# Linear attention with a gated FFN on one core: later loads held behind the first tile, eps on POOL, the last sum in two halves, and another search for the order

## The chip, the cores and the metric

The kernel runs on one core of one Trainium2 chip. The metric is the device time of an execution in microseconds, here the median of several runs. The engines are TensorE (PE, with its weight loads shown apart as PEld), VectorE (DVE), ScalarE (ACT), GpSimd (POOL) and SyncE (SP), which issues all DMAs.

## The reference

```python
xn = layernorm(A_x)                              # 2048 x 512, eps 1e-5
q, k, v = split(xn @ A_wqkv)                     # 32 heads of 16
pq, pk = phi(q), phi(k)                          # where(t > 0, t + 1, exp(t)) + 1e-6
kv = sum_s pk^T v ; z = sum_s pk                 # per head
o = (pq @ kv) / (pq . z + 1e-6)
s = o @ A_wo
g = silu((gelu(xn @ w_gate) * (xn @ w_up)) @ w_down)   # 512 -> 1792 -> 512
y = A_x + s * g
```

All is float32. (The FFN's input is the normalised x as well.)

## The kernel before

**Tiles.** The 2048 rows are 16 tiles of 128 tokens (`x`, normalised `xn`, transposed on PE into the bank `pt`). Each number is split into a high part that PE takes in its fast float format (a cast on ACT: `Xh`, `kq`, `xnh`, `hh`, `dwh`) and a low rest (a subtraction on DVE: `Xl`, `kq`, `xnl`, `hl`, `dwl`); a product is then three matmuls, `mm3`, lines 364 to 366. The larger products run by a scheme with seven block products instead of eight (`prod`, `fprod`), whose sums of blocks (`T`, `tmp`) are made on POOL.

**Stages.** (1) Normalise, transpose, products for k and q, `phi` of both; q is written to `q_d`, and `gacc` gathers pk and xn into the four banks `gps`. The first four tiles use plain products (`plain`), later ones the scheme. (2) From about 118 us the FFN of the second half of the tokens (`quad`, banks `FX`, `FY`, `FZ`), whose down products go to the banks `d` and are added to `acc` in groups of units (`down`). (3) From about 330 us the attention part: `kv`, `pm`, and for each of 16 tiles a transpose `ptq`, a cast `pqTh` and the product `sps`. (4) From about 410 us the FFN of the first half, and at the end `finish0`: silu of `acc`, times `s` (tile `fs`, loaded from `s_d`), plus x (tile `fx`), and the store.

**What sets the order.** Nothing is issued while the code runs: `do` records each operation with its engine, an estimated duration and what it must wait for. `Plan.order` then puts them in sequence. PE's order is written by hand as a list of keys (`pe_keys`), from which the planner may run ahead by 6 us (`AHEAD`). From PE's turn each operation gets a latest time `late`; `forward` goes through the program and takes on each engine the ready operation with the smallest `late`. Then 400 rounds (`ROUNDS`) shift `late` at random around one of PE's planned waits and keep what doesn't end later. The result is one fixed order for each engine, so a waiting instruction holds up everything behind it on its engine; SP's DMAs stand in one queue too.

**The first tile.** `load_next` and `dma` queue x and wqkv by turns: the first x tile, half of `wk1`, the second x tile, and so on, none waiting for anything. `ln` makes the statistics (`st`, `mv`) on DVE, adds eps (`ve`, line 504) on DVE, raises to -0.5 on POOL (`rstd`, line 506) and normalises on DVE (line 510). PE runs 15 warm-up matmuls on ones, then the transposes.

**The end.** The last tile's sum (`j == 7`) is made by 12 matmuls of 512 columns into one bank; DVE then adds it to `acc` in two halves of 256 columns, and silu, product and addition of x follow by halves. For tiles 0 to 5 the addition of x stands on POOL, for 6 and 7 on DVE.

## Time and profile before

| what | us |
|---|---|
| runs | 632.27, 632.03, 629.70 (median 632.03) |
| the profiled execution | 629.64, its span 627.6 |
| PE busy in the span | 616.1 |
| DVE, ACT, POOL busy | 422.2, 321.2, 247.9 |

A row of the timeline gives the start, the duration, the engine, the line and the operation, and in brackets how long the engine had been idle and what ended that. The ends of matmuls are modelled: in an unbroken row one starts every 0.227 us though each is shown with 0.39. Busy time of PE therefore tells little; the idle time and the steps between starts tell where it waited. A table by stretches gives for each window its length and the busy time of PE, PEld, DVE, ACT and POOL.

### The profile page before, as it was taken

To read this page: it belongs to the slowest core of one execution; us is meant where nothing else is said; L and a number is where in the kernel's file an instruction comes from. 1 tells how busy PE (TensorE), PEld (TensorE's weight loads), DVE (VectorE), ACT (ScalarE), POOL (GpSimd) and SP (SyncE) were. 2 spreads that over 40 slices of the span, in tenths; PEclk is the share of its full clock that TensorE was granted. 3 is DMA by queue.
4 is the path that set the end of the run, shared out by engine and by line. 5 is a ranking of instruction groups with operands and counts; after the bars stand their busy time and mean duration, and the time that the engine had idled before them with its cause. 6 is when DMAs were issued, how large, how long until landed. Compare 5 with 4: busy or idle time off the path is not lost.

```text
span 627.6 us, 7822 instructions
## 1 busy us (share of the span) xinstructions
PE 616.1 (98%) x2780; PEld 506.0 (81%) x2780; DVE 422.2 (67%) x644; ACT 321.2 (51%) x571; POOL 247.9 (40%) x243
## 2 busy tenths in 40 slices
PE   7999999999999999999999999999999999999995
PEld 6878788888888888888888787888888888888884
DVE  6999998688746743762459689967566527723554
ACT  6677777797565622650345322266656316612431
POOL 2465554456644530360035433135534404300142
PEclk9999999999999999999999999999999999999999
DMA  6239921136121210220069544872221202000173
GB/s 239 80 124 299 298 68 38 65 102 201 44 72 54 56 46 34 67 68 0 34 201 359 199 131 148 289 251 67 68 65 36 68 34 68 0 1 34 34 206 130
DMA packets 52439, 68.67 MB, mean 109 GB/s; under 512 B 2864, under 2 KB 31792, under 8 KB 52400
## 3 DMA queue, kind: packets, MB, share of 16 engines
q1 hardware_dynamic: 52400, 68.17, 33.9%
q8 instruction: 22, 0.36, 0.2%
q14 instruction: 17, 0.14, 0.1%
HBM read 49.28 MB, written 18.87 MB: 109 GB/s over the span
## 4 chain that ended last, share of the span: by engine, by line
PE 94%; DVE 3%; ACT 1%; issue 0%; POOL 0%; DVEq 0%; ACTq 0%; POOLq 0%
PE FX L364 8%; PE FX L365 8%; PE FX L366 8%; PE d L365 8%; PE d L366 8%; PE d L364 8%; PE FZ L365 4%; PE FZ L366 4%; PE FZ L364 4%; PE sps L366 2%; PE sps L364 2%; PE sps L365 2%; PE gps L366 2%; PE gps L364 2%; PE gps L365 2%; PE FY L365 2%
## 5 line engine op out<-in xcount | busy, mean ns | idle before, releaser
L847 POOL TENSOR_TENSOR h<-h,g 128x512 f32<-128x512 f32 x42 | 62.1, 1477 | 173.3 <-DVE h L356 173.3
L364 PE MATMUL d<-dwh,hh 128*128 128x512 f32 x224 | 87.8, 392 | 0.0
L364 PE MATMUL FX<-Xh,w 128*128 128x512 f32 x224 | 87.5, 391 | 0.1
L366 PE MATMUL FX<-Xh,w 128*128 128x512 f32 x224 | 87.2, 389 | 0.0
L366 PE MATMUL d<-dwh,hl 128*128 128x512 f32 x224 | 87.2, 389 | 0.0
L365 PE MATMUL d<-dwl,hh 128*128 128x512 f32 x224 | 87.2, 389 | 0.0
L365 PE MATMUL FX<-Xl,w 128*128 128x512 f32 x224 | 87.2, 389 | 0.0
L356 POOL TENSOR_TENSOR tmp<-raw 128x256 f32<-128x256 f32 x56 | 49.1, 890 | 85.1 <-DVE w L356 70.3
L885 DVE TENSOR_TENSOR acc<-acc,d 128x512 f32<-128x512 f32 (+1 forms) x49 | 32.8, 674 | 52.5 <-PE d L366 52.1
L350 ACT COPY fu<-FX 128x512 f32<-128x512 f32 x56 | 32.9, 587 | 54.3 <-PE FX L366 53.7
L350 ACT CAST hh<-h 128x512 fp32r<-128x512 f32 x56 | 34.5, 620 | 46.4 <-PE d L365 27.0
L364 PEld LDWEIGHTS FX<-Xh,w 128*128 128x128 f32 x224 | 42.0, 188 | 10.0 <-ACT fu L350 1.4
L364 PEld LDWEIGHTS d<-dwh,hh 128*128 128x128 f32 x224 | 42.1, 188 | 8.9 <-issue 0.2
L365 PEld LDWEIGHTS d<-dwl,hh 128*128 128x128 f32 x224 | 42.1, 188 | 8.8 <-issue 0.2
L366 PEld LDWEIGHTS d<-dwh,hl 128*128 128x128 f32 x224 | 42.0, 188 | 8.7
L366 PEld LDWEIGHTS FX<-Xh,w 128*128 128x128 f32 x224 | 42.0, 188 | 8.7
L365 PEld LDWEIGHTS FX<-Xl,w 128*128 128x128 f32 x224 | 42.0, 188 | 8.7
L356 DVE TENSOR_TENSOR w<-tmp,w 128x512 fp32r<-128x512 f32 x56 | 42.0, 772 | 9.8 <-ACT w L350 9.8
L356 DVE TENSOR_TENSOR w<-raw,w 128x512 fp32r<-128x512 f32 (+1 forms) x56 | 45.7, 825 | 3.2 <-ACT w L350 3.2
L356 DVE TENSOR_TENSOR hl<-h,hh 128x512 fp32r<-128x512 f32 x56 | 41.2, 735 | 5.6 <-ACT hh L350 5.6
L364 PE MATMUL FZ<-Xh,w 128*128 128x512 f32 x112 | 43.6, 389 | 0.0
L365 PE MATMUL FZ<-Xl,w 128*128 128x512 f32 x112 | 43.6, 389 | 0.0
(186 smaller groups left out, 1396.8 us busy)
## 6 DMA issues: line engine op xcount, KB each, us to landing
raw<-in_B_w_gate SPq DMA_DIRECT2D x14, 512.0 KB, 3.8
raw<-in_B_w_up SPq DMA_DIRECT2D x14, 512.0 KB, 3.8
draw<-in_B_w_down SPq DMA_DIRECT2D x14, 512.0 KB, 3.3
x<-in_A_x SPq DMA_DIRECT2D x16, 256.0 KB, 3.3
q_d<-qp SPq DMA_DIRECT2D x16, 256.0 KB, 2.2
q<-q_d SPq DMA_DIRECT2D x16, 256.0 KB, 3.0
xh_d<-Xh SPq DMA_DIRECT2D x4, 896.0 KB, 5.9
xl_d<-Xl SPq DMA_DIRECT2D x4, 896.0 KB, 6.4
```

The costliest lines, as they stand in the source:

```text
L350: do("ACT", act(n), lambda o, i: nc.scalar.copy(o, i), dst, src, name=name)
L356: do(eng, c, lambda o, p, q: getattr(e, f"tensor_{op}")(o, p, q), dst, a, b, name=name)
L364: nc.tensor.matmul(ps, wh, mh, start=start, stop=False, skip_group_check=on)
L365: nc.tensor.matmul(ps, wh, ml, start=False, stop=False, skip_group_check=on)
L366: nc.tensor.matmul(ps, wl, mh, start=False, stop=stop, skip_group_check=on)
L847: do("POOL", pool(NC), lambda o, i: nc.gpsimd.tensor_mul(o, o, i), h, g, name="h")
L885: do("DVE", dve(D // n), lambda o, i: nc.vector.tensor_add(o, o, i), acc[p, j][cl], ps[cl], name="acc")
```

## The change

Four edits go together.

1. **Loads.** Only the first x tile, the first half of the k weights (`wk1`) and the second x tile are issued at once. Every later load of the start first has one column of its target overwritten by a copy on POOL (`hold`) from the first tile's statistics, so that the load must wait for these.
2. **eps.** The addition of eps (`ve`) moves from DVE to POOL, for all tiles.
3. **The last sum.** In the last group of the FFN of the first half the tile `j == 7` is made in two halves of 256 columns, each in a bank of its own, with 24 matmuls of 256 columns; the views of `acc` and `fs` have two parts, so that each half is waited for by itself. The addition of x is on DVE for all tiles.
4. **The search.** Instead of 400 rounds, a table (`KEPT`) lists stretches of PE's turn and the seeds that are applied there; a round shifts `late` either along the chain that held up one wait (`chain`) or around it.

```diff
-ROUNDS = 400
+KEPT = [
+    (-1, 12, [300008, 300085, 300320, 300352]),
+    (12, 25, [300005]),
...
+    (605, 9999, [300017, 300018, 300031]),
+]
...
+        for lo, hi, draws in KEPT:
+            for n in draws:
+                best = self.altered(n, lo, hi, pe, *best)
+        return [o for _, o in best[1]]
+
+    def altered(self, n, lo, hi, pe, _, done, late):
+        draw = random.Random(n)
+        for o in self.ops:
+            o.late = late[o]
+        waits = [w for w in self.waits(done) if lo <= w[0] < hi]
+        if not waits:
+            return _, done, late
+        w = draw.choices(waits, [w[1] for w in waits])[0]
+        if draw.random() < 0.5:
+            for o in self.chain(done, w[2]):
+                if draw.random() < 0.7:
+                    o.late -= draw.uniform(0.0, 4.0)
...
+        new = self.forward(pe)
+        return max(t for t, _ in new), new, {o: o.late for o in self.ops}
...
-        do("DVE", 0.1, lambda o, i: nc.vector.tensor_scalar_add(o, i, EPS_LN), ve, mv[:, :, 1])
+        do("POOL", 0.1, lambda o, i: nc.gpsimd.tensor_scalar_add(o, i, EPS_LN), ve, mv[:, :, 1])
...
+    load_next()
+    for k in range(2):
+        dma(half(wk1, k), ext(wqkv_k[:, k, D:2 * D]), 256)
+    load_next()
+
+    t0 = tokens[0][0]
+    mv0 = ln_stats(t0)
+
+    def hold(v):
+        do("POOL", 0.1, lambda o, i: nc.gpsimd.tensor_copy(o, i), v, mv0[:, 0, 0:1], name="hold")
+
+    for k in range(2):
+        hold(half(wk2, k)[:, 0:1])
+        dma(half(wk2, k), ext(wqkv_k[:, 2 + k, D:2 * D]), 256)
+    for _ in range(2):
+        t = xq.pop(0)
+        xs[t] = U("x", range(0, 4), f"x{t}")
+        hold(xs[t][:, 0:1])
+        dma(xs[t], ext(x[t * P:(t + 1) * P, :]), 256)
...
+    ln(t0, mv=mv0)
...
+    def halves(p, units_, j):
+
+        return 2 if p == 0 and units_ == groups[-1] and j == 7 else 1
...
+            for c in range(m):
+                ps = bank(ring("down", [5, 6, 7]), f"d{p}_{units_[0]}_{j}{c}", (P, D // m))
+                cs = slice(c * D // m, (c + 1) * D // m)
...
-            tt("POOL" if j < 6 else "DVE", "add", sr[cl], sr[cl], xr[cl], w)
+            tt("DVE", "add", so, so, xr[:, i * w:(i + 1) * w], w)
```

What this does to the order is seen in the built programs, at three places.

**The start, POOL.** Before, from the last of the set-up to the third power (`mask` belongs to the attention, `rstd` is the root of the variance):

```order
L382 MEMSET zacc 128x512
L955 MEMSET mask_114 128x128
L956 AFFINE_SELECT mask_114<-mask_114 128x128
L506 TENSOR_TENSOR rstd_145<-ve_142,neg_half 128x1
L506 TENSOR_TENSOR rstd_172<-ve_167,neg_half 128x1
L506 TENSOR_TENSOR rstd_231<-ve_226,neg_half 128x2
```

And now, behind the same set-up:

```order
L539 COPY wk_133<-mv_126 128x1
L521 TENSOR_SCALAR ve_135<-mv_126 128x1
L539 COPY wk_133<-mv_126 128x1
L523 TENSOR_TENSOR rstd_139<-ve_135,neg_half 128x1
L539 COPY x_142<-mv_126 128x1
L539 COPY x_149<-mv_126 128x1
L539 COPY wq_152<-mv_126 128x1 x2
L539 COPY wq_168<-mv_126 128x1 x2
L521 TENSOR_SCALAR ve_180<-mv_176 128x1
L523 TENSOR_TENSOR rstd_185<-ve_180,neg_half 128x1
```

Two copies and the addition stand between the first statistics and the first root, and six copies between the first and the second root.

**The start, DVE.** Before, from the first statistics:

```order
L501 BN_STATS st_134<-x_95 128x6
L502 BN_AGGR mv_140<-st_134 128x2
L504 TENSOR_SCALAR ve_142<-mv_140 128x1
L510 TENSOR_SCALAR xn_149<-x_95,mv_140,rstd_145 128x512
L501 BN_STATS st_152<-x_110 128x6
L502 BN_AGGR mv_163<-st_152 128x2
L504 TENSOR_SCALAR ve_167<-mv_163 128x1
L356 TENSOR_TENSOR Xl_170<-pt_154,Xh_165 128x2x128 x2
L510 TENSOR_SCALAR xn_177<-x_110,mv_163,rstd_172 128x512
L356 TENSOR_TENSOR kq_175<-wk_106,kq_175 128x512 x2
```

And now:

```order
L513 BN_STATS st_124<-x_95 128x6
L514 BN_AGGR mv_126<-st_124 128x2
L527 TENSOR_SCALAR xn_144<-x_95,mv_126,rstd_139 128x512
L403 TENSOR_TENSOR kq_146<-wk_113,kq_146 128x512
L513 BN_STATS st_165<-x_118 128x6
L514 BN_AGGR mv_176<-st_165 128x2
L403 TENSOR_TENSOR Xl_178<-pt_154,Xh_163 128x2x128 x2
L403 TENSOR_TENSOR kq_146<-wk_113,kq_146 128x512
L403 TENSOR_TENSOR kq_146<-wk_133,kq_146 128x512
L513 BN_STATS st_200<-x_142 128x6
L527 TENSOR_SCALAR xn_205<-x_118,mv_176,rstd_185 128x512
```

The first low half of the weights (`kq`) now stands ahead of the second tile's statistics, and the second tile's `xn` behind two more of them and the third tile's statistics. PE's second transpose, which needs that `xn`, stood ahead of all products and now stands behind nine matmuls of the first tile.

**At 44 us, DVE.** Before, around the last `phi` of q (`qp`), whose bank PE's product `Y` takes next:

```order
L356 TENSOR_TENSOR kq_204<-wk_106,kq_204 128x1024
L356 TENSOR_TENSOR kq_259<-s_1_420,kq_204 128x512
L356 TENSOR_TENSOR kq_259<-s_0_430,kq_204 128x512
L356 TENSOR_TENSOR kq_259<-wq_138,kq_259 128x1024
L591 SCALAR_TENSOR_TENSOR qp_557<-q_520,qr_547 128x512
L356 TENSOR_TENSOR Xl_170<-pt_512,Xh_165 128x2x128
```

And now:

```order
L403 TENSOR_TENSOR kq_207<-wk_113,kq_207 128x1024
L657 SCALAR_TENSOR_TENSOR qp_566<-q_524,qr_556 128x512
L403 TENSOR_TENSOR Xl_178<-T_550,Xh_163 128x4x128
L403 TENSOR_TENSOR kq_274<-s_0_434,kq_207 128x512
L403 TENSOR_TENSOR kq_274<-s_1_442,kq_207 128x512
L403 TENSOR_TENSOR kq_274<-wq_152,kq_274 128x1024
```

`qp` has moved ahead of three of the low halves of the weights.

**The end, PE and DVE.** PE near 596 us, before, between the third and the last product into the bank `FX`:

```order
L366 MATMUL FX_5300<-Xh_3776,w_5009 128x512
L364 MATMUL d_5_0_5374<-dwh_5_5195,hh_25_5132 128x512
L365 MATMUL d_5_0_5374<-dwl_5_5200,hh_25_5132 128x512
L366 MATMUL d_5_0_5374<-dwh_5_5195,hl_25_5137 128x512
L364 MATMUL FX_5300<-Xh_3776,w_5009 128x512
```

And now:

```order
L413 MATMUL FX_5312<-Xh_3769,w_5019 128x512
L411 MATMUL d_5_00_5382<-dwh_5_5203,hh_25_5140 128x512
L412 MATMUL d_5_00_5382<-dwl_5_5208,hh_25_5140 128x512
L413 MATMUL d_5_00_5382<-dwh_5_5203,hl_25_5145 128x512
L411 MATMUL d_5_00_5382<-dwh_5_5203,hh_25_5280 128x512
L412 MATMUL d_5_00_5382<-dwl_5_5208,hh_25_5280 128x512
L413 MATMUL d_5_00_5382<-dwh_5_5203,hl_25_5290 128x512
L411 MATMUL FX_5312<-Xh_3769,w_5019 128x512
```

Six matmuls of a down product stand there instead of three. DVE at the very end, before:

```order
L885 TENSOR_TENSOR acc_6_4286<-acc_6_4286,d_5_6_5534 128x512
L1069 TENSOR_TENSOR fs_5490<-fs_5490,acc_6_4286 128x512
L356 TENSOR_TENSOR fs_5490<-fs_5490,fx_5468 128x512
L885 TENSOR_TENSOR acc_7_4311<-acc_7_4311,d_5_7_5552 128x256 x2
L1069 TENSOR_TENSOR fs_5505<-fs_5505,acc_7_4311 128x256
L356 TENSOR_TENSOR fs_5505<-fs_5505,fx_5487 128x256
```

And now:

```order
L956 TENSOR_TENSOR acc_6_4295<-acc_6_4295,d_5_60_5528 128x512
L403 TENSOR_TENSOR fs_3969<-fs_3969,fx_5425 128x512
L1139 TENSOR_TENSOR fs_5501<-fs_5501,acc_6_4295 128x512
L956 TENSOR_TENSOR acc_7_4308<-acc_7_4308,d_5_70_5559 128x256
L403 TENSOR_TENSOR fs_5501<-fs_5501,fx_5483 128x512
L956 TENSOR_TENSOR acc_7_4308<-acc_7_4308,d_5_71_5575 128x256
L1139 TENSOR_TENSOR fs_5517<-fs_5517,acc_7_4308 128x256
L403 TENSOR_TENSOR fs_5517<-fs_5517,fx_5491 128x256
```

The two halves of the last sum are separate now, with the addition of tile 6 between them, and the addition of tile 5 has come over from POOL.

More of the change, by code (lines that the diff above doesn't have):

```diff
@@ L70 @@
 class Op:
-    __slots__ = ("eng", "cost", "lat", "fn", "pre", "suc", "key", "late", "end", "left", "ready", "name", "turn", "port", "kb", "lat0")
+    __slots__ = ("eng", "cost", "lat", "fn", "pre", "suc", "key", "late", "end", "left", "ready", "name", "turn", "port", "kb", "lat0", "no")
 class Plan:
@@ L928, in ffn @@
         assert len(todo) == 1
-        return keys, lambda j: [("D", p, u, j, i) for u in todo[0] for i in range(2)]
+        return keys, lambda j: [("D", p, u, j, i, c) for c in range(halves(p, todo[0], j)) for u in todo[0] for i in range(2)]
     keys1, last1 = ffn(1, lambda p, j: silu(p, j))
```

138 lines of the change are left out of this document (79 added, 59 removed).

## The prediction

> **What bounds the kernel now.** I read the page's head first, then busy times by stretch, then the timeline of PE and the rows around its gaps.
>
> ```profile
> span 627.6 us, 7822 instructions
> PE 616.1 (98%) x2780; PEld 506.0 (81%) x2780; DVE 422.2 (67%) x644; ACT 321.2 (51%) x571; POOL 247.9 (40%) x243
> ...
> 5.00:20.00 15.00, 12.53 (x66) 9.81 (x66) 13.90 (x30) 12.96 (x27) 4.71 (x5) 1.00 0.60 216
> 20.00:44.00 24.00, 23.61 (x108) 19.18 (x106) 23.29 (x42) 16.93 (x31) 14.20 (x13) 1.00 0.29 92
> 44.00:65.00 21.00, 20.43 (x93) 16.19 (x94) 19.63 (x33) 14.46 (x27) 8.23 (x10) 1.00 0.93 282
> ```
>
> PE is the bound: 11.5 us of the span lie outside its busy time, and only these can be won, since no matmul is taken away. In the three stretches (length, then busy PE, PEld, DVE, ACT, POOL) DVE works 56.8 of 60 us: up to 65 us DVE is as tight as PE, and a wait of PE there is work that DVE did too late.
>
> The gaps of PE inside the program, by timeline (start, duration; the bracket is the idle time and what ended it):
>
> ```profile
> 43.41 0.68 DVE L591 SCALAR_TENSOR_TENSOR qp<-q,qr 128x512 f32<-128x512 f32 x1
> ...
> 44.14 0.50 PE L364 MATMUL Y<-kq,Xh 128*128 128x512 f32 x1 [0.53 <-DVE qp L591]
> ...
> 64.05 0.67 DVE L356 TENSOR_TENSOR Xl<-T,Xh 128x512 fp32r<-128x512 f32 x1
> ...
> 64.78 0.50 PE L366 MATMUL X<-kq,Xl 128*128 128x512 f32 x1 [0.43 <-DVE Xl L356]
> ...
> 326.92 0.39 PE L366 MATMUL d<-dwh,hl 128*128 128x512 f32 x1
> ...
> 327.36 0.50 PE L364 MATMUL FX<-Xh,w 128*128 128x512 f32 x1
> ...
> 388.97 0.50 PE L364 MATMUL sps<-M_hi,pqTh 128*128 128x512 f32 x1 [0.29 <-ACT pqTh L350]
> ...
> 596.33 0.59 ACT L350 COPY fu<-FX 128x512 f32<-128x512 f32 x1 [2.13 <-PE FX L366]
> ...
> 596.53 0.39 PE L366 MATMUL d<-dwh,hl 128*128 128x512 f32 x1
> ...
> 596.97 0.50 PE L364 MATMUL FX<-Xh,w 128*128 128x512 f32 x1
> ```
>
> A matmul starts every 0.227 us in an unbroken row (eleven steps from 618.18 to 620.68, quoted with the tail). So the waits are 0.53, 0.43, 0.21 (327.36 less 326.92 and 0.227), 0.29 and 0.21 us. The rest of the 11.5 us is the start and the tail.
>
> **Part 1, the start.** What stands there now:
>
> ```profile
> 3.41 0.69 DVE L501 BATCH_NORM_STATS2 st<-x 128x6 f32<-128x512 f32 x1 [2.35 <-DMA x<-in_A_x]
> ...
> 4.14 0.18 DVE L502 BATCH_NORM_AGGREGATE mv<-st 128x2 f32<-128x6 f32 x1
> ...
> 4.60 0.56 POOL L506 TENSOR_TENSOR rstd<-ve,neg_half 128x1 f32<-128x1 f32 x1 [1.79 <-DVE ve L504]
> ...
> 5.19 0.55 DVE L510 TENSOR_SCALAR xn<-x,mv,rstd 128x512 f32<-128x512 f32 x1 [0.68 <-POOL rstd L506]
> ...
> 6.06 0.60 PE L522 MATMUL pt<-ident,xn 128*128 128x128 f32 x4
> ...
> 6.23 0.69 DVE L501 BATCH_NORM_STATS2 st<-x 128x6 f32<-128x512 f32 x1 [0.49 <-DMA x<-in_A_x]
> ...
> 6.70 0.65 ACT L350 CAST Xh<-pt 128x256 fp32r<-128x256 f32 x2 [0.31 <-PE pt L522]
> ...
> 8.64 0.66 PE L522 MATMUL pt<-ident,xn 128*128 128x128 f32 x4 [1.98 <-DVE xn L510]
> ...
> 12.76 0.70 POOL L506 TENSOR_TENSOR rstd<-ve,neg_half 128x2 f32<-128x2 f32 x1 [4.78 <-DVE ve L504]
> ...
> 13.00 0.50 PE L366 MATMUL k<-kq,b 128*128 128x512 f32 x1 [0.49 <-DVE b L356]
> ...
> 13.34 0.40 PE L364 MATMUL k<-kq,b 128*128 128x512 f32 x1
> ...
> 14.10 0.66 PE L522 MATMUL pt<-ident,xn 128*128 128x128 f32 x4
> ...
> x<-in_A_x SPq DMA_DIRECT2D x16, 256.0 KB, 3.3
> ```
>
> PE idles 1.98 us for the second transpose, which now stands ahead of every product; in the change nine matmuls of the first tile stand ahead of it. Row 13.34 gives a second price: after a wait the next matmul follows after 0.34 instead of 0.227 us, so each wait costs 0.11 more.
>
> The added work is on POOL. Between the aggregate and the power stand two hold copies and the eps addition, then six more copies. No such operation is in the trace, so I bound it. From below:
>
> ```profile
> 56.56 0.74 POOL L356 TENSOR_TENSOR T<-xt,T 128x256 f32<-128x256 f32 x1
> ...
> 612.44 1.29 POOL L356 TENSOR_TENSOR fs<-fs,fx 128x512 f32<-128x512 f32 x1 [1.49 <-DVE fs L1069]
> ```
>
> 256 columns more cost 0.55 us, so what does not depend on columns is 0.74 - 0.55 = 0.19 us. From above, the only one-column operation with inputs, the power, took 0.56. A copy is nearer to the fixed part: I take 0.19. The aggregate ends at 4.32; with 0.09 us to POOL, three operations of 0.19 and the power of 0.56 the root is ready at 5.54, and xn starts at 5.57 instead of 5.19. That 0.38 us hides behind the warm-up matmuls, which hold the first transpose at 6.06 to 6.2 as before. The held loads (second half of wk, two x tiles, wq) leave later, but wk2 is cast only after 8 us. The third x tile queues behind a load that waits for xn and is issued near 6.6; at 3.3 us to land (the page's median for x) it is there before its statistics at about 11.2.
>
> DVE by steps of 0.60 (512 columns), 0.34 (256) and 0.45 (xn) then has: low half of kq 6.0, statistics of the second tile 6.6 (not waited for: fewer loads fly beside it), Xl 7.4, kq 8.1, kq 8.9 (after ACT's cast), statistics 9.5, second xn 10.1 to 10.64. The transpose goes at 10.7 and the first block of products ends near 11.8; the next has its wait for b until 12.3 instead of 13.0. But the third transpose needs the root of two tiles, now with the addition on POOL: aggregate to 12.3, 0.19 + 0.70, xn 13.35 to 13.9, transpose at 13.95 instead of 14.10. Of the 1.98 us PE gets 0.15 at this point, and about 0.4 two blocks later, because the fourth transpose fits between products. I take **-0.3** (bounds -0.8, with the additions at nothing, to +1.2, with 0.56 each, worked out below).
>
> **Part 2, the order up to 65 us.** At 44 DVE did three low halves of kq ahead of qp, whose bank Y needs; in the change qp stands ahead of them and 44.14 is not waited for. At 64.78 two xn, xnl, c, kp and statistics preceded Xl; one xn of 0.45 is gone from there. Together the two waits are 0.53 + 0.43 + 2 x 0.11 = 1.18 us. DVE's work is the same but for the eps additions, so some of it is late elsewhere: I take **-0.8** (bounds -1.2 and +0.5, another wait like the largest of these).
>
> **Part 3, PE's own order later.** At 596 PE put three matmuls between the last product into FX and the next; they last 0.68 us, while the copy fu needs the bank until 596.92. The change puts six there (1.36 us), which covers it. At 327 another product of six stands between. At 388 two transposes stood back to back with their cast behind them; one now stands thirteen rows earlier. These waits are 0.21 + 0.29 + 0.21 + 3 x 0.11 = 1.04 us; I take **-0.9** (bounds -1.04 and 0).
>
> **Part 4, the tail.**
>
> ```profile
> 618.18 0.39 PE L364 MATMUL d<-dwh,hh 128*128 128x512 f32 x1
> ...
> 618.38 0.69 DVE L885 TENSOR_TENSOR acc<-acc,d 128x512 f32<-128x512 f32 x1 [0.64 <-PE d L366]
> ...
> 619.83 0.69 DVE L1069 TENSOR_TENSOR fs<-fs,acc 128x512 f32<-128x512 f32 x1 [0.76 <-ACT acc L895]
> ...
> 620.55 0.69 DVE L356 TENSOR_TENSOR fs<-fs,fx 128x512 f32<-128x512 f32 x1
> ...
> 620.68 0.39 PE L366 MATMUL d<-dwh,hl 128*128 128x512 f32 x1
> ...
> 621.17 0.74 DVE L885 TENSOR_TENSOR acc<-acc,d 128x256 f32<-128x256 f32 x2
> ...
> 623.37 0.42 DVE L356 TENSOR_TENSOR fs<-fs,fx 128x256 f32<-128x256 f32 x1
> ...
> 13.11 0.19 PEld L364 LDWEIGHTS k<-kq,b 128*128 128x128 f32 x1
> ...
> 349.91 3.59 PE L991 MATMUL pm<-mstuff 128*128 128x512 f32 x8
> ```
>
> Twelve matmuls of 512 columns become 24 of 256, each with its own weight load. Two loads can start 0.11 us apart (one goes with 13.00, the next at 13.11), half a matmul streams 0.11, so I take 0.12 each: the last starts at 618.18 + 23 x 0.12 = 620.94 and is done at 621.22. DVE decides, not PE. It now does the sixth tile's addition too (at 619.00, in a free place), the product at 619.83, first half 620.45, addition 620.82, second half 621.42, then product, addition, product, addition at 621.79, 622.25, 622.60 and 623.05, the last 0.32 us ahead of 623.37: **-0.3**. If the 0.19 us of a load cannot overlap with itself, the second half waits until 622.8 and the end is 1.1 us later than now.
>
> [...] No run here shows half-width products yet.
>
> **The sum.** -0.3 - 0.8 - 0.9 - 0.3 = -2.3 us. An order that was not run before will also make waits, and I allow one short one, +0.3: **-2.0**. The profiled execution took 629.64 (span 627.6 and 2.0 around it), which gives 627.6. The other three took 632.27, 632.03 and 629.7: two levels 2.4 us apart, which the trace doesn't explain. I set the change against the mean of the four, 630.9: **628.9 us**; on the median alone it would be 630.0.
>
> **The rivals.** *The waits only move* (chance 0.28): DVE is 95% busy to 65 us, so parts 1 and 2 give nothing and parts 3 and 4 remain: -0.9 - 0.3 + 0.3 = -0.9, 630.0. For it speaks the busy table, against it the plainly non-urgent statistics and kq that stood ahead of urgent rows.
>
> *Holding the loads doesn't help and delays the first tile* (0.14): it lands by 3.41 either way, since its load is first in the queue. With 0.56 us for each small POOL operation xn starts 3 x 0.37 = 1.1 us later than I have it, the third transpose another 0.37, DVE has no slack to make it good: part 1 is +1.2, part 2 nothing, the sum 1.2 - 0.9 - 0.3 + 0.3 = +0.3, 631.2. It loses from about 0.5 us an operation on.
>
> *Half-width products don't run at half the time* (0.06): the slow side. The fp32 products pm took 3.59 / 8 = 0.45 us for 512 columns in each of two passes, 0.45 for 256 in both. At that pace the last half-width matmul starts at 618.18 + 23 x 0.45 = 628.5; the tail is 7.0 us longer and the sum -2.0 + 0.3 + 7.0 = +5.3, 636.2. It turns the whole change slower from about 0.22 us a matmul on, that is when half a width costs as much as a whole one. Against it: products of this type stream 512 columns in 0.227.
>
> *Everything comes* (0.10): all parts at their good bounds, -0.8 - 1.2 - 1.0 - 0.4 = -3.4, 627.5. The forecast keeps 0.42.
>
> **How the numbers follow.** About 0.5%, 3.2 us, is what a measurement of this kernel can tell. Counted from the median 632.03, faster begins at 628.9: half of the forecast, the good case, and a sixth of the moved waits, together 0.38. Slower is the half-width case and a little of the delayed start, 0.08; the rest is 0.54. The range goes from below the good case with the lower level, 626.8, to the delayed start with the upper, 632.6.
>
> **What would show it.** Right: the second transpose of PE no longer has idle time before the first product, no wait is left at qp, at 327, 388 and 597, and the last half-width matmul starts less than 2.9 us after the first. Wrong: small POOL rows of half a microsecond between aggregate and power; DVE idle for a load near 7 or 11 us; new brackets of over 0.3 us on PE between 20 and 130 us; half-width matmuls 0.19 us or more apart; more than 0.1 us lost between PE's end and the last addition.

## The result, and the profile after

The changed kernel took 632.65 us (median of 22 runs, 631.81 to 633.44), the kernel before 631.92 (22 runs beside them, 629.70 to 633.07): a ratio of 1.0017, 95% interval 1.0009 to 1.0026. It is a little slower, and 3.8 us over the forecast of 628.9; the median lies just above the range. In the figures of this document one run of 691.02 us (three moves) and one of 3571.7 us (the kernel before) are left out, since they stand far from all others of their kernels. The profiled execution took 633.17 us, with this head of its page:

```profile
span 631.4 us, 7862 instructions
...
PE 619.1 (98%) x2792; PEld 507.8 (80%) x2792; DVE 427.3 (68%) x641; ACT 320.3 (51%) x571; POOL 244.4 (39%) x254
```

Twelve more matmuls (halves at the end), eleven more rows on POOL. The span is 3.8 us longer than in the first profile of before, and PE is again the bound. The busy times by stretch (length, PE, PEld, DVE, ACT, POOL):

```profile
5.00:20.00 15.00, 12.55 (x60) 9.19 (x60) 11.12 (x23) 10.06 (x21) 5.25 (x14) 1.00 0.65 216
20.00:44.00 24.00, 24.00 (x111) 19.84 (x111) 22.78 (x42) 18.72 (x34) 16.07 (x17) 1.00 0.30 92
44.00:65.00 21.00, 20.66 (x96) 16.46 (x95) 20.76 (x32) 13.92 (x26) 7.98 (x9) 1.00 0.80 234
```

At the start DVE is no longer tight (11.1 of 15 us, 13.9 before): it now has idle time of its own. PE's timeline has the rest:

```profile
7.36 0.60 PE L588 MATMUL pt<-ident,xn 128*128 128x128 f32 x4
...
10.83 0.50 PE L412 MATMUL k<-kq,Xh 128*128 128x512 f32 x1 [0.94 <-DVE kq L403]
12.49 0.66 PE L588 MATMUL pt<-ident,xn 128*128 128x128 f32 x4 [0.22 <-DVE xn L527]
...
16.34 0.66 PE L588 MATMUL pt<-ident,xn 128*128 128x128 f32 x4 [0.59 <-DVE xn L527]
...
24.12 0.39 PE L411 MATMUL q<-a,Xh 128*128 128x512 f32 x1
...
59.19 0.50 PE L411 MATMUL X<-kq,Xh 128*128 128x512 f32 x1 [0.34 <-DVE qp L657]
...
82.80 0.50 PE L411 MATMUL X<-kq,Xh 128*128 128x512 f32 x1 [0.20 <-ACT u L397]
...
107.76 0.50 PE L411 MATMUL X<-kq,Xh 128*128 128x512 f32 x1 [0.42 <-DVE qp L657]
...
140.04 0.50 PE L411 MATMUL FX<-Xh,w 128*128 128x512 f32 x1 [0.98 <-DVE qp L657]
...
421.04 0.50 PE L411 MATMUL FX<-Xh,w 128*128 128x512 f32 x1 [0.83 <-ACT fu L397]
```

The waits of before at 44, 64, 389 and 597 us are gone. In their place are the five last rows, from 59 us on, at places where the profile of before marks no wait. The first transpose starts at 7.36 us, 6.06 in the first profile of before, although its input is ready by 6.31.

Since two runs differ in where they start, I count PE's idle time from its first transpose on: each matmul's start less the start of the one ahead, less 0.227 us for 512 columns (0.12 for 256, 0.09 for each piece of a transpose), summed by stretch. The stretch 165 to 440 us holds some 3 us in every kernel for steps of other shapes. The second column of numbers is the first transpose's start, the last is what is left of the span, the tail among it (span less all columns ahead, less 609 us of work).

| kernel | span | first transpose | to 24 us | 24-72 | 72-100 | 100-165 | 165-440 | 440-610 | left |
|---|---|---|---|---|---|---|---|---|---|
| before, first profile | 627.6 | 6.06 | 3.68 | 2.64 | 0.46 | 0.49 | 3.91 | 0.32 | 1.0 |
| before, second profile (below) | 630.0 | 7.37 | 4.80 | 2.64 | 0.35 | 0.61 | 3.89 | 0.36 | 1.0 |
| changed | 631.4 | 7.36 | 4.44 | 1.52 | 1.64 | 2.77 | 4.05 | 0.00 | 0.6 |
| three moves | 628.9 | 6.69 | 4.44 | 1.63 | 1.59 | 1.50 | 3.36 | 0.01 | 0.7 |
| middle of before | 628.4 | 6.26 | 4.42 | 2.16 | 0.65 | 0.46 | 4.70 | 0.05 | 0.7 |
| middle, moves, no hold | 625.6 | 6.39 | 3.32 | 2.15 | 0.67 | 0.39 | 3.04 | 0.06 | 0.6 |

So the change wins 1.1 us from 24 to 72 us, 0.3 at the end of the middle part and 0.4 in the tail, and loses 1.2 to 1.3 us from 72 to 100 and 2.2 to 2.3 from 100 to 165 us. Between 165 and 440 us a gain and a loss cancel. The start is 0.4 us better or 2.1 worse, by which profile of before it is held against. Most of the 2.1 is the later first transpose; behind it PE is idle 0.76 us more than in the first profile and 0.36 less than in the second.

### The profile page after: what moved, and what is told of

Its sections match the earlier page's. It is cut to its first block, busy times and chain, and to the rows that moved or that the text cites. A ratio compares the mean times of both kernels' runs of the same rounds, so it can differ in the third digit from the quotient of the medians.

```text
span 631.4 us, 7862 instructions
## 1 busy us (share of the span) xinstructions
PE 619.1 (98%) x2792; PEld 507.8 (80%) x2792; DVE 427.3 (68%) x641; ACT 320.3 (51%) x571; POOL 244.4 (39%) x254
## 4 chain that ended last, share of the span: by engine, by line
PE 73%; DVE 2%; ACT 1%; DMA 1%; issue 1%; POOLq 0%; DVEq 0%
PE FX L411 8%; PE FX L413 8%; PE FX L412 8%; PE d L413 7%; PE d L411 7%; PE d L412 7%; PE FZ L411 4%; PE FZ L413 4%; PE FZ L412 4%; PE sps L413 2%; PE sps L411 2%; PE sps L412 2%; PE FY L413 2%; PE FY L411 2%; PE FY L412 2%; PE ptq L1088 1%
## 5 line engine op out<-in xcount | busy, mean ns | idle before, releaser
L411 PE MATMUL d<-dwh,hh 128*128 128x512 f32 (+1 forms) x228 | 88.4, 388 | 0.0
L413 PE MATMUL d<-dwh,hl 128*128 128x512 f32 (+1 forms) x228 | 87.9, 385 | 0.0
L412 PE MATMUL d<-dwl,hh 128*128 128x512 f32 (+1 forms) x228 | 87.9, 385 | 0.0
L403 POOL TENSOR_TENSOR tmp<-raw 128x256 f32<-128x256 f32 x56 | 44.4, 809 | 78.4 <-DVE w L403 62.8
L403 DVE TENSOR_TENSOR w<-raw,w 128x512 fp32r<-128x512 f32 (+1 forms) x56 | 48.4, 874 | 5.4 <-ACT w L397 5.4
L403 DVE TENSOR_TENSOR hl<-h,hh 128x512 fp32r<-128x512 f32 x56 | 44.4, 793 | 7.2 <-ACT hh L397 7.0
L411 PE MATMUL FZ<-Xh,w 128*128 128x512 f32 x112 | 43.7, 390 | 0.0
L413 PE MATMUL FZ<-Xh,w 128*128 128x512 f32 x112 | 43.6, 389 | 0.0
```

The costliest lines, as they stand in the source:

```text
L403: do(eng, c, lambda o, p, q: getattr(e, f"tensor_{op}")(o, p, q), dst, a, b, name=name)
L411: nc.tensor.matmul(ps, wh, mh, start=start, stop=False, skip_group_check=on)
L412: nc.tensor.matmul(ps, wh, ml, start=False, stop=False, skip_group_check=on)
L413: nc.tensor.matmul(ps, wl, mh, start=False, stop=stop, skip_group_check=on)
```

## The experiments

All medians below may be set against 632.65: the lowest run of the kernel before was between 629.51 and 629.75 us in each of the five sets of runs, so the chips agree within 0.3 us, while its median went from 630.4 to 631.9 with the share of its two levels.

**The kernel before, profiled again.** No edit.

> The kernel before, unchanged, profiled a second time, because its times fall on two levels, about 629.7 and 632.3, and its trace shows only the lower one. Theory one (the levels are two starts: the warm-up matmuls run 0.21 us a record until the pace doubles, at a moment that differs from run to run, and the first transpose waits for them): a run near 632 shows the first transpose 1.3 us or more later than 6.06 and a lower mean clock, and from 20 us on PE keeps this distance to the first trace within 0.3 us; a run near 629.7 shows it at 6.0 to 6.2. Theory two (the levels come from later waits, a load or a bank): the first transpose is at 6.1 in either and PE falls behind at a place after 20 us.

The run took 632.09 us, the upper level. Its PE timeline at the start:

```profile
7.37 0.60 PE L522 MATMUL pt<-ident,xn 128*128 128x128 f32 x4
9.95 0.71 PE L522 MATMUL pt<-ident,xn 128*128 128x128 f32 x4 [1.98 <-DVE xn L510]
10.36 0.73 PE L364 MATMUL k<-kq,Xh 128*128 128x512 f32 x1
10.88 0.63 PE L365 MATMUL k<-kq,Xh 128*128 128x512 f32 x1
11.31 0.63 PE L366 MATMUL k<-kq,Xl 128*128 128x512 f32 x1
```

and the windows of 7 to 12 and 12 to 24 us (the number ahead of the last two is the granted clock), first of this run, then of the first profile:

```profile
7.00:12.00 5.00, 3.02 (x17) 2.54 (x16) 3.32 (x7) 4.00 (x10) 0.56 (x1) 0.84 1.01 365
12.00:24.00 12.00, 11.95 (x51) 9.16 (x51) 10.67 (x22) 9.78 (x20) 3.96 (x3) 0.92 0.18 55
```

```profile
7.00:12.00 5.00, 3.36 (x17) 2.87 (x18) 4.92 (x11) 5.00 (x12) 0.56 (x1) 1.00 1.04 395
12.00:24.00 12.00, 11.51 (x54) 8.83 (x53) 11.65 (x26) 10.42 (x21) 5.29 (x4) 1.00 0.17 58
```

The first transpose is 1.31 us later, and after PE's pause of 1.98 us the products start 0.43 us apart instead of 0.227, at a granted clock of 0.84 and then 0.92. By the first q product PE is 2.44 us behind, and it stays 2.4 to 2.5 behind to the end. The two levels are two starts, as theory one had it; of the 2.44 us, 1.31 are the later first transpose (the warm-ups take 6.41 us; 5.11 in the first profile, where they start 0.213 us apart up to 4.39 us and 0.112 from there on), and the rest goes with the lower clock after the pause, where theory one looked for it in the warm-ups alone. The times on record bear this out: of the 108 runs of before for which they give the granted clock, the 58 with 0.998 or 0.999 over the whole run took 629.51 to 631.31 us, the 50 with 0.995 or 0.996 took 631.61 to 633.10. Against the median of the first group (630.1) the changed kernel is 2.5 us slower, against that of the second (632.5) about as fast. The profile that the prediction was made from was of the better start.

**The old search on the new steps.** The table of draws goes, the 400 rounds of before come back.

```diff
-        for lo, hi, draws in KEPT:
-            for n in draws:
-                best = self.altered(n, lo, hi, pe, *best)
+        draw = random.Random(1)
+        for n in range(ROUNDS):
...
```

> The changed kernel with one part undone: the order comes from the search of before (400 draws over the whole run), and held loads, additions on POOL and the tail in halves stay. Theory one (the new order wins 1.4 us to 70 us and about 1 us at 327 to 600, but loses 3.8 us between 70 and 170 us and 0.85 us at 421, by waits of PE for DVE and ACT that it made itself): this order has the product's low half of wd behind qp and c at 140 us, so that wait of 1.15 us is gone, and the qp of 44 us is ahead as in the change; the time is 629.5 to 631.5, at least 1 us below the changed kernel. Theory two (the loss comes from what all orders share, the held loads, the smaller steps on POOL and the clock): the time is that of the changed kernel, 632.65 within 0.5 us.

633.54 us (632.37 to 635.24, ratio to before 1.003, interval 1.0017 to 1.0044). The wait at 140 us fell to 0.25, but others came (1.58 at 12 us, 0.80 at 61, 0.55 at 102), and the one at 421 stayed. Neither theory: the new search is 0.9 us better than the old one on these steps, so the loss is not that a worse search took the place of a better one.

**No hold.** The eight copies are planned but emit nothing.

```diff
-        do("POOL", 0.1, lambda o, i: nc.gpsimd.tensor_copy(o, i), v, mv0[:, 0, 0:1], name="hold")
+        do("POOL", 0.1, lambda o, i: None, v, mv0[:, 0, 0:1], name="hold")
```

> The changed kernel without the hold copies: the later loads leave at once, while PE, DVE, ACT and the order stay word for word; eight one-column copies are gone from POOL. Theory one (the first tile is first in its queue and lands as soon either way; xn waited 0.35 us longer for two more copies, but the warm-up matmuls hold the first transpose): the first statistics start at 3.4 to 3.7 us as in both kernels, the root is ready 0.2 us (one copy row) or more earlier, the second tile lands later or as soon, and the time is within 0.4 us of the changed kernel. Theory two (the held loads make room): the first statistics start 0.3 us or more later and the time is 0.5 us or more longer. Theory three (the hold is what made the start slower): the first q product is 1 us or more earlier than 24.1, and the time 1 us shorter.

632.71 us (632.12 to 633.96): the same. The first statistics start at 3.46 us instead of 3.70, so holding the later loads does not bring the first tile sooner. Theory one.

**eps on DVE.**

```diff
-        do("POOL", 0.1, lambda o, i: nc.gpsimd.tensor_scalar_add(o, i, EPS_LN), ve, mv[:, :, 1])
+        do("POOL", 0.1, lambda o, i: nc.vector.tensor_scalar_add(o, i, EPS_LN), ve, mv[:, :, 1])
```

> The changed kernel with eps added on DVE again, in the same place of the order: DVE has one small row more for each root, POOL one less; PE, ACT and the loads stay. Theory one (an addition of one or two columns costs either engine about 0.2 us, so DVE has 8 x 0.1 to 0.2 us more in the first 90 us, and the hop between the engines is the same): within 0.5 us of the changed kernel, rather longer, 0 to +0.5 us. Theory two (POOL's step is what delays xn and the third transpose): the root chain from aggregate to xn is 0.2 us shorter or more, and the time 0.3 to 0.8 us shorter.

633.45 us (632.97 to 634.43): 0.8 longer. The start is not where it shows. PE waits for xn at 49 us (0.25) and at 63 us, where the changed kernel has no wait,

```profile
63.03 0.63 PE L588 MATMUL pt<-ident,xn 128*128 128x128 f32 x4 [0.53 <-DVE xn L527]
```

and 0.92 instead of 0.42 at 108; the wait of 0.34 at 59 us is gone. Nine such rows of about 0.15 us stand on DVE, some 1.4 us in all, and a little over half of that reaches the kernel's time; DVE is busy 96% of the time from 44 to 100 us. Taking them off DVE is a real gain of the change in this order, of which the prediction counted nothing.

**Three moves.** Four steps of the planned order are moved by hand (step, ahead of or behind which).

```diff
+MOVES = [(819, False, 629), (888, False, 819), (488, True, 483), (1575, True, 1573)]
...
-    for o in plan.order(pe_keys):
+    turn = plan.order(pe_keys)
+    for n, ahead, m in MOVES:
+        o, to = plan.ops[n], plan.ops[m]
+        turn.remove(o)
+        turn.insert(turn.index(to) + (not ahead), o)
+    for o in turn:
         o.fn()
```

DVE of the changed kernel at 138 us, with the low half of wd (dwl) ahead of the row that PE waits for:

```profile
137.56 0.68 DVE L657 SCALAR_TENSOR_TENSOR qp<-c,qr 128x512 f32<-128x512 f32 x1
138.17 1.21 DVE L403 TENSOR_TENSOR dwl<-draw,dwh 128x1024 fp32r<-128x1024 f32 x1
139.30 0.68 DVE L657 SCALAR_TENSOR_TENSOR qp<-X,qr 128x512 f32<-128x512 f32 x1
```

and ACT at 419 us, with the table load and gelu ahead of the copy that empties bank FX:

```profile
418.59 1.28 ACT L885 ACT_TABLE_LOAD   x1
419.88 0.63 ACT L885 ACTIVATE g<-g 128x512 f32<-128x512 f32 x1
420.42 0.57 ACT L397 COPY fu<-FX 128x512 f32<-128x512 f32 x1
```

dwl is first used at 177 us, gelu's result by POOL several microseconds later; neither had to be there.

> The changed kernel with four rows of its order moved by hand and nothing else: at 140 us the 1.2 us low half of wd on DVE goes behind qp and c (and the load that waits for it behind it), at 107 us the qp out of bank X goes ahead of the qp out of c, and at 421 us ACT copies fu out of the bank ahead of the table load and gelu. Theory one (each of the three rows alone holds PE at its wait: 1.15 + 0.11, 0.58 + 0.11 and 0.99 + 0.11 us by the trace of the changed kernel, of which 0.1 to 0.2 us each may stay): 2.0 to 2.9 us less than the changed kernel, about 630.1, and PE has no idle time over 0.25 us at these three places. Theory two (DVE and ACT have no slack there, so what is moved comes back as another wait within 30 us): the three brackets are gone but others of the same sum stand behind them, and the time is within 0.7 us of the changed kernel.

630.38 us (629.65 to 631.38), 2.27 less than the changed kernel; ratio to before 0.998, interval 0.9967 to 0.9994. On DVE:

```profile
137.41 0.69 DVE L657 SCALAR_TENSOR_TENSOR qp<-X,qr 128x512 f32<-128x512 f32 x1 [0.35 <-ACT qr L655]
138.01 0.68 DVE L403 TENSOR_TENSOR c<-u,Z 128x512 f32<-128x512 f32 x1
138.61 1.22 DVE L403 TENSOR_TENSOR dwl<-draw,dwh 128x1024 fp32r<-128x1024 f32 x1
```

The brackets at 107 and 421 us are gone, the one at 140 us (now at 138) is 0.28, and no others came. Theory one: each of these three waits was made by one row.

**Two readers of a bank.** Nothing changes place on any engine; only in the program's text DVE's low halves come ahead of ACT's plain copy out of the same bank.

```diff
+MOVES = [(76, True, 72), (95, True, 91)]
```

In the changed kernel DVE's second half waits for that copy, though it does not use it:

```profile
9.76 0.43 DVE L403 TENSOR_TENSOR Xl<-pt,Xh 128x256 fp32r<-128x256 f32 x1 [0.65 <-ACT xt L397]
10.10 1.28 DVE L403 TENSOR_TENSOR kq<-wk,kq 128x512 fp32r<-128x512 f32 x2
...
14.07 0.42 DVE L403 TENSOR_TENSOR b<-pt,b 128x256 fp32r<-128x256 f32 x1 [0.37 <-ACT xt L397]
```

> The changed kernel with two rows moved in the program's text only: the low halves that DVE takes out of a transposed tile's bank are issued ahead of ACT's plain copy out of the same bank. No engine's own order changes; what changes is which of two readers of a bank waits for the other. Theory one (in the changed kernel DVE waits 0.65 us at 9 us and 0.37 us at 13 us for that copy by ACT, which it has no need of, and the low half of kq behind it holds PE at 10.8 us for 0.94 us): DVE's two waits are gone, PE's wait at 10.8 us is 0.4 us or more shorter and the time 0.3 to 0.9 us less than the changed kernel. Theory two (ACT's copy now waits for DVE instead, and the two casts of kq behind it on ACT are late by as much): the wait at 10.8 us stays within 0.2 us and so does the time.

632.22 us (631.19 to 632.93), 0.43 less. That is little more than the 0.3 us by which the chips agree, but in the trace PE's idle time to 24 us is 0.5 less too. Both halves now run in a row, and another wait of DVE came behind them, for a cast that ACT now does later:

```profile
8.00 0.76 DVE L403 TENSOR_TENSOR Xl<-pt,Xh 128x256 fp32r<-128x256 f32 x2 [0.69 <-ACT Xh L397]
8.67 0.68 DVE L403 TENSOR_TENSOR kq<-wk,kq 128x512 fp32r<-128x512 f32 x1
9.92 0.69 DVE L403 TENSOR_TENSOR kq<-wk,kq 128x512 fp32r<-128x512 f32 x1 [0.58 <-ACT kq L397]
```

PE's wait of 0.94 us became two of 0.20 and 0.22. Theory one, at the lower end, with theory two's loss in part.

**More moves.** The three, and others at 9 to 13, 58, 82 and 140 us.

```diff
+MOVES = [..., (72, False, 37), (91, False, 93), (111, True, 95), (262, True, 256), (263, True, 248), (405, True, 399), (818, False, 625)]
```

> The three moves of the earlier run (at 107, 140 and 421 us) and further ones of the same kind: at the start ACT's two plain copies of transposed tiles go behind the casts that DVE and PE wait for and behind DVE's reads of the same bank, and one aggregate goes ahead of a low half; at 58 us the exponent of bank X goes ahead of the linear part of c and its qp ahead of a low half of pk; at 82 us the copy u goes ahead of an exponent; at 140 us the cast of wd also goes behind the exponents. Theory one (waits of PE can be taken away singly, since DVE and ACT each have slack within 2 us of them): the start gains 0.8 to 1.5 us against the run with three moves, and the places at 58, 82 and 140 us 0.2 to 0.5 each: 628.0 to 629.3, faster than both kernels. Theory two (up to 90 us DVE works without a break, so PE's waits only change their place): within 0.6 us of the run with three moves, 630.4.

630.30 us (629.82 to 631.17): theory two by the time. By the stretches both have a part. To 24 us PE is idle 3.35 us instead of 4.44, but from 72 to 100 us 2.73 instead of 1.64: with the copy u ahead of an exponent at 82 us, PE then waits 0.77 for pkl at 84 and 0.81 for Xl at 88 us.

**The tail undone.** The last product in one piece, its sums still in halves.

```diff
-                            mm3(o, hh[:, sl], hl[:, sl], dh[:, i, cs], dl[:, i, cs], st, sp)
+                            if c == 0:
+                                mm3(o, hh[:, sl], hl[:, sl], dh[:, i, :], dl[:, i, :], st, sp)
```

> The changed kernel with one part undone: the last tile's product is taken in one piece of 512 columns again (12 matmuls for 24 halves), and the order of everything else stays. Theory one (the halves let the last additions start 1.3 us sooner, but DVE, with 2.7 us of work for each of the last tiles, is late and gives most of it back): 0.3 to 0.6 us slower than the changed kernel. Theory two (DVE alone sets the end): within 0.2 us. Theory three (the extra weight loads cost more than the halves win): faster by 0.3 us or more.

633.30 us (632.54 to 634.06): 0.65 slower. The halves win, a little more than theory one's middle. In the changed kernel they run 0.12 us apart, as the prediction took them, first and last of the row on PE:

```profile
622.49 0.28 PE L411 MATMUL d<-dwh,hh 128*128 128x256 f32 x1
622.60 0.28 PE L412 MATMUL d<-dwl,hh 128*128 128x256 f32 x1
...
625.24 0.28 PE L413 MATMUL d<-dwh,hl 128*128 128x256 f32 x1
```

and DVE's last addition starts at 627.38, 1.9 us behind PE's end:

```profile
622.88 0.68 DVE L956 TENSOR_TENSOR acc<-acc,d 128x512 f32<-128x512 f32 x1
...
627.38 0.42 DVE L403 TENSOR_TENSOR fs<-fs,fx 128x256 f32<-128x256 f32 x1
```

From the last tile's first matmul to the start of the last addition it is 4.89 us, 5.19 before: 0.30 less. With the product in one piece it is 5.43.

**Without the draws for 70 to 100 us.**

```diff
-    (70, 85, [300015, 300019, 300027]),
-    (85, 100, [300002]),
```

> The changed kernel without the search's four draws for PE's waits between 70 and 100 us of its own count; the other draws, the held loads, POOL's additions and the tail stay. Without them the low half of wd stands behind qp and c at 140 us, the qp out of bank X ahead of that out of c at 107 us, and the copy u ahead of the exponent at 82 us, as in no other part of the change. Theory one (these four draws, made for waits near 85 us, put the rows there that hold PE at 82, 107 and 140 us): 1.5 to 2.6 us less than the changed kernel, 630.0 to 631.2; the wait at 421 us stays. Theory two (they also took waits away, as they were drawn to do, and both sides cancel): within 0.6 us of the changed kernel, with new waits at 75 to 100 us.

636.45 us (636.18 to 636.63): 3.8 slower, beyond what theory two allowed. PE now waits 1.25 us at 78 us, and further on at 118, 137, 147 and 341:

```profile
78.57 0.50 PE L411 MATMUL X<-kq,Xl 128*128 128x512 f32 x1 [1.25 <-DVE Xl L401]
```

The four draws made the three bad rows, and yet are worth 3.8 us: about 2 us of the idle time that came without them lies behind 165 us. A new order up to 100 us shifts all rows behind it, so a single draw cannot be judged at its own place.

**The best so far, and fewer warm-ups.** The three moves, those at the start and the cast of wd; then the same with 7 matmuls for 11 in the first warm-up group, and the kernel before with 7.

```diff
+MOVES = [(819, False, 629), (888, False, 819), (818, False, 625), (488, True, 483), (1575, True, 1573), (72, False, 37), (91, False, 93), (111, True, 95)]
```

```diff
-WARM = 11
+WARM = 7
```

> The moves that paid so far, together: the three (107, 140 and 421 us), the start's (ACT's plain copies behind the casts and behind DVE's reads, the aggregate ahead of a low half), and ACT's cast of wd behind the exponents at 140 us; those at 58 and 82 us are left out. Theory one (the start's moves win 1.1 us by 24 us, as the run with more moves showed, and what that run lost between 82 and 90 us came from the copy u alone): 628.7 to 629.6. Theory two (what the start wins is lost again by 100 us wherever it came from, since DVE sets the pace there): 630.0 to 630.6, as with three moves.

> The run before this one with 7 instead of 11 matmuls in the first group of warm-ups, so 11 in all. Theory one (the warm-ups hold the first transpose, at 6.6 to 7.5 us in the kernels with the change, while its input is ready at 6.3; PE keeps what it gains there): the transpose starts at 6.2 to 6.5 us and the time is 0.4 to 1.0 us less than with 11. Theory two (PE's pace doubles only after so many microseconds of work, and with fewer warm-ups the first products run at the slow pace): the transpose is earlier but the first products are not, and the time is the same within 0.3 us or longer.

> The kernel before with 7 instead of 11 matmuls in the first group of warm-ups. In its second profile, of a run on the upper level, the granted clock was 0.84 from 7 to 12 us and 0.92 from 12 to 24 us, the first transpose stood at 7.37 and PE was 2.45 us behind from 25 us to the end. Theory one (both levels come from how long the warm-ups hold PE): with eleven in all the first transpose is at 6.1 in every run, and all times lie within 0.8 us near 629.7. Theory two (the levels are the granted clock after the warm-ups, whatever their number): two levels stay, 2 us or more apart.

With the moves 629.71 us (628.92 to 630.81), the same with 7 warm-ups 629.58 (629.08 to 630.66), before with 7 warm-ups 631.35 (630.05 to 632.55). The moves at the start gave 0.7 us rather than 1.1. The profiled run took 630.81, the longest of the twelve, so its trace shows more loss than the median has. DVE now comes to the third tile before the tile is there:

```profile
11.34 0.69 DVE L513 BATCH_NORM_STATS2 st<-x 128x6 f32<-128x512 f32 x1 [1.22 <-DMA x<-in_A_x]
```

The second xn stands behind these statistics, so PE pauses for it, and behind the pause the granted clock is low here too, 0.57 in the window of 12 to 16 us:

```profile
12.53 1.12 PE L588 MATMUL pt<-ident,xn 128*128 128x128 f32 x4 [1.63 <-DVE xn L527]
```

```profile
12.00:16.00 4.00, 3.47 (x11) 2.96 (x12) 3.40 (x10) 2.44 (x6) 0.94 (x2) 0.57 0.73 258
```

With 7 warm-ups the first transpose is 0.6 us sooner but takes 1.11 us instead of 0.60, so the first product starts at 7.67 instead of 7.75; DVE waits 0.62 us for the same load. PE is no further by 24 us than in the run with more moves, and the time is the same, as theory two had it. For before neither theory holds: nine of twelve runs lie above 631.2, between the levels or on the upper one, and the profile shows the lowest granted clock of all:

```profile
7.00:12.00 5.00, 3.44 (x10) 2.90 (x11) 4.96 (x11) 4.54 (x11) 0.56 (x1) 0.58 1.04 396
```

With fewer warm-ups PE had worked less before its pause of 2.06 us at the second transpose: its 11 warm-up matmuls take 4.26 us, the 15 of before 5.11 and 6.41 in the two profiles. Over the whole run the granted clock was 0.996 or less in nine of these twelve runs and in 50 of the 108 with the full warm-up. Whether it is the warm-ups that decide the clock behind that pause, twelve runs and one profile do not show.

**The middle of before.** From 72 to 172 us the order of before for the same 467 steps, the change's order ahead and behind.

```diff
+MID = [310, 312, 441, 442, 376, ...]
...
-    for o in plan.order(pe_keys):
+    turn = plan.order(pe_keys)
+    mid = [plan.ops[n] for n in MID]
+    turn = turn[:339] + mid + [o for o in turn[339:] if o not in set(mid)]
```

> The changed kernel with its own order to 72 us and from 172 us on, and in between the order of the kernel before for the same 467 steps. Theory one (the waits between 72 and 165 us, 4.4 us of idle PE in the changed kernel where before had 1.0, come from that stretch's order alone): nearly all of it goes, PE's idle time between 72 and 165 us is under 1.5 us and the time 629.3 to 630.0. Theory two (DVE, 96% busy from 44 to 100 us, takes back by 100 us what PE wins before 72 us, in whatever order, and only the waits at 107 and 140 us belong to the order): PE is idle 1.2 us or more between 72 and 100 us, and the time is 630.2 to 631.0.

630.22 us (629.68 to 630.97), 2.4 less, ratio to before 0.9983, interval 0.9971 to 0.9995. The first product of the last stage, which waited until 140.04 in the changed kernel, waits no more:

```profile
136.68 0.39 PE L411 MATMUL FX<-Xh,w 128*128 128x512 f32 x1
```

The time lies in theory two's range. From 72 to 165 us PE is idle 1.1 us instead of 4.4, as theory one asked. But 0.6 us of it came back just ahead of 72, where the two orders meet: from 24 to 100 us the sum is 2.8 us, 3.2 in the changed kernel and 3.0 to 3.1 in before. Up to 100 us theory two is nearer: it comes to about 3 us with each of these orders (not with every order: about 2.5 with the old search, 4.1 with more moves). From 100 to 165 us it is the order alone, 0.46 for 2.77.

**The middle of before with the moves, and without the hold.**

```diff
+MOVES = [(72, False, 37), (91, False, 93), (111, True, 95), (1575, True, 1573)]
```

> The run before this one with the moves at the start (ACT's two plain copies behind the casts and DVE's reads, the aggregate ahead of a low half) and the copy fu ahead of the table load at 421 us. Theory one (gains at places apart add up): 1.0 to 2.0 us less than that run, about 628.3, the shortest of all. Theory two (the start's gain is lost by 100 us): 0.8 to 1.0 us less, the wait at 421 us alone.

> The run before this one without the hold copies. With the start's moves DVE comes to the third tile's statistics sooner, and in two of three profiles it waited 0.6 and 1.2 us there for that tile's load. Theory one (the hold delays the loads ahead of it in the queue, so without it the tile is there sooner): no such wait, and 0.3 to 0.8 us less. Theory two (that load waits for its place in a buffer, not for the hold): the same within 0.3 us.

628.40 us (627.64 to 628.93), and without the hold 627.62 (627.22 to 628.29). The first is 1.8 us under the run before it. In the trace PE is idle 1.0 us less to 24 us and the same from 24 to 100 us, so the start's gain lasts, and the wait at 421 us is gone. The second is the shortest of all, ratio to before 0.9943, interval 0.9924 to 0.9962, 5.0 us under the changed kernel. Its place in the table is the last row, and on PE's timeline:

```profile
135.66 0.39 PE L411 MATMUL FX<-Xh,w 128*128 128x512 f32 x1
```

That leaving out the hold wins 0.8 us here and nothing in the changed kernel fits theory one, a load that comes late only where DVE comes early. But there are six runs of each, whose ranges overlap, and the two traces do not show the cause (neither waits for the load, and the spans differ by 0.3 us): why the hold costs time here stays open.

## Why the prediction failed, point by point

The step that failed is the last line of its sum: "An order that was not run before will also make waits, and I allow one short one, +0.3". These waits came to about 4.5 us: 1.3 between 72 and 100 us, 2.2 between 100 and 165, and 1.1 at 421 us (0.99 and the 0.11 behind it), counted against the second profile of before. Three of the terms that should win came, a little larger than written: the order to 65 us -1.1 (forecast -0.8), PE's own order about -0.8 from 360 to 395 us and -0.3 at 597 (forecast -0.9 in all), the tail -0.4 in the table and 0.65 by the run that undid it (-0.3).

The start is the other term that failed. Against the second profile it is -0.4 (forecast -0.3), but only because before lost time there to a lower clock, of which the prediction knew nothing: the near agreement is luck. Against the first profile, from which the term was worked out and whose clock stayed at 1.00 as the changed kernel's did, PE is idle 0.76 us more behind the first transpose. With the second profile as base, the four terms make about -3.0, against -2.3 in the sum, and with +4.5 about the 1.4 us between the spans of 631.4 and 630.0.

Of the 3.75 us between forecast and result, 1.0 is the base: 630.9 was the mean of four runs, 631.92 the median of 22. The rest is the change itself, forecast at -2.0 and measured at +0.7. (The profiled run of the changed kernel lies 0.5 us above its median, so the spans differ by a little more.)

**The start.** The second transpose no longer leaves PE idle before the first product, and the small POOL rows ahead of the first root took 0.18 to 0.23 us, near the 0.19 of the prediction:

```profile
4.68 0.18 POOL L539 COPY wk<-mv 128x1 f32<-128x1 f32 x1 [1.87 <-DVE mv L514]
4.83 0.23 POOL L521 TENSOR_SCALAR ve<-mv 128x1 f32<-128x1 f32 x1
5.01 0.19 POOL L539 COPY wk<-mv 128x1 f32<-128x1 f32 x1
5.15 0.58 POOL L523 TENSOR_TENSOR rstd<-ve,neg_half 128x1 f32<-128x1 f32 x1
```

Wrong was that the warm-ups hold the first transpose "at 6.06 to 6.2 as before": in the kernels with the change and the full warm-up it started at 6.26 to 7.50 us, by the run. Wrong too was that the third transpose comes at 13.95: it came at 16.34. Of the 2.39 us, 1.30 are the later first transpose; most of the rest are DVE's two waits, 0.65 and 0.37, for ACT's reads of the same bank, which the order of rows per engine does not show. The second tile's statistics did not wait for their load, as forecast, but not because fewer loads flew beside it: the tile landed at 6.2 us in the first profile of before (4.5 us from its issue at 1.71) and at 6.3 in the changed kernel (4.1 from 2.17); DVE came to it at 6.83 instead of 6.23. And the profile was of the better of two starts; the prediction saw two levels and could not place them.

**The order to 65 us.** The waits at 44 and 64 us went as forecast. The bound on the bad side, "another wait like the largest of these", was drawn for the same 20 us; what was late came due behind them. The rival in which the waits only move had it right for 24 to 100 us, where PE's idle time is 3.0 to 3.1 us before and 3.2 after.

**PE's own order.** Six matmuls did cover the copy at 597 us, and the wait at 389 went; at 327 nothing was won (1.0 us of idle time from 325 to 360 us in both). That the term came out even so is because the stretch around 389 gave about 0.8 us, not the 0.40 counted for the wait there. What was not looked for is the same kind of copy at the beginning of the last stage, on ACT. In before it stood ahead of the table load,

```profile
415.10 0.59 ACT L350 COPY fu<-FX 128x512 f32<-128x512 f32 x1 [0.22 <-PE FX L366]
415.71 1.28 ACT L820 ACT_TABLE_LOAD   x1
```

and the change's order puts load and gelu first, as quoted with the three moves: the wait at 421 us.

**The tail.** Mechanism and size were right. DVE decides, the last start is 0.30 us nearer to the last tile's first matmul, and half-width matmuls are 0.12 us apart, so the rival of the slow halves falls.

**The hold.** It does nothing for the first tile, whose statistics start at 3.70 us with it and at 3.46 without, as that rival had it; its price of 0.56 us for each small row was wrong.

## What to carry to other kernels

Where a change replaces an order by a search, list the rows of the new order that stand ahead of each bank's release on every engine, in all stretches, not only where the old waits were: three such rows cost 2.3 us here. They were found by the trace; no run shows that the order alone would have told them from harmless rows. Measure the whole order as well: the four draws that made two of these rows were worth 3.8 us together. In a stretch where one engine is busy 96% of the time, as DVE is here from 44 to 100 us, allow for new waits as large as the old ones. Before a sum is made against one profile, find out whether the kernel's times lie on one level or two, and which of them the profile shows.

## What was not expected of the hardware

A pause of PE of 2 us soon after its warm-up cost more than itself in some runs. In the second profile of before the products behind the pause of 1.98 us start 0.43 us apart instead of 0.227, at a granted clock of 0.84 from 7 to 12 us; with fewer warm-ups, behind 2.06 us, the clock was 0.58 in that window. After a pause of 1.63 us, in the profiled run with all moves that paid, it was 0.57 from 12 to 16 us. The changed kernel, whose longest wait there is 0.94 us, ran at 1.00, and its runs spread over 1.6 us, not 3.4. A long pause does not always do it: the first profile of before, with the same 1.98 us, stayed at 1.00, and the profiled run of the old search, with 1.58, had 0.999 as a whole. What decides it, no run here shows.

The warm-up matmuls change their pace too, and not at the same time in each run: they start 0.213 us apart at first and then 0.112, from 4.39 us on in the first profile of before, from 7.02 in that of the changed kernel.

Two engines that read the same bank were kept apart by the order in which the program's text names them: DVE waited 0.65 us for a copy by ACT whose result it did not use, and moving the text alone took that wait away. Why they are kept apart, no run here shows.

Small rows on an engine that is busy 96% of the time were not free: with eps on DVE, nine rows of about 0.15 us made the kernel 0.8 us longer, a little over half of their own time, and the waits of PE stand at 49, 63 and 108 us, apart from the rows themselves.
